# New planner settings for attention scores, value products and feed-forward sums past the opening

## The chip, the core and the metric

The kernel runs on one core of a Trainium2 chip. The metric is the device time of one execution in microseconds, the median of three runs. Beside it stands the profile of one execution, whose span runs from the first to the last instruction of the program.

## The reference

The program computes attention with normalised queries and keys and feeds the result into a multiplicative feed-forward network. There are 8 batches, 12 heads, 448 positions and 64 numbers per head; inputs are float32.

```
q_n = q / rms(q) * g_q ;  k_n = k / rms(k) * g_k
scores = q_n @ k_n.T / 8 ;  attn = softmax(scores) ;  o = attn @ v        # per head
x = o, with the 12 heads of a token side by side                          # 3584 x 768
h = (x @ w1) * (x @ w2) @ w3                                              # 3584 x 1024
out = h @ w_out                                                           # 3584 x 768
```

Nothing but a matrix product follows the multiplication of the two products, so the kernel computes w3 @ w_out once, calls it `w34s`, and multiplies by it.

## The kernel before

**Units of attention.** The work is cut into 24 units i of four heads each, three units to a batch. A unit goes through these steps. Its q and k are loaded (`load_qk`, L367, into one of three buffers). ScalarE squares them (`sq`, L464), VectorE sums the squares (L471), ScalarE takes a logarithm and an exponential for the inverse root (L480, L483), VectorE scales q and k by it (`scale`, L494; `by_g`, L503). For units 0 to 4 TensorE transposes the result; from unit 5 on a DMA issued by SyncE does it (`send`, L561). Then come seven score steps (`do_score`, L679): four 64x64-tile matmuls of 448 columns into two PSUM banks each, and one exponential on ScalarE over both banks (L701). I write S9.2 for step 2 of unit 9 on TensorE, and E9.2 for its exponential. When all seven exponentials of a unit, or of two units together, are done and v has landed, the value products run (`start_pv`, `do_pv_rest` L745, `do_pv_main` L766): per unit one sum of weights, whose reciprocal ScalarE takes as a logarithm and an exponential (`pv_summed`, L788 and L789), and two blocks of values, which VectorE multiplies by that reciprocal into `xT` (L808).

**Feed-forward.** When three units have filled `xT` of a batch, eight pairs of sums are queued for it: products with w1 (here A) and with w2 (here B). An A pair is copied to SBUF by ScalarE or VectorE (`half`, L352 or L358); the B pair is multiplied by that copy on VectorE (L949, into `abT`). The tiles of two batches are then multiplied by `w34s` (here O) and copied out and stored. A pair holds two PSUM banks and consists of twelve (A, B) or sixteen (O) passes; a pass (`do_pass`, L868) is four matmuls of 64x64 tiles that run side by side. Halfway through a pair the two row halves of the array swap banks. Before that swap a small instruction on SyncE or GpSimd (`hand_over`, L852) must have seen the first half end; if no other pass or score stands between the halves, TensorE waits for it.

**What sets the order.** The kernel is written by a planner while it is built. `Planner.run` keeps an estimated clock for each engine and a list of jobs with a duration, a key and conditions; on each engine the job that can start first, and among those the one with the lowest key, is written next. TensorE's next step is chosen by `pe_try`: value products first if `pv_size` allows them and enough banks are idle, then the running pair, a score if ScalarE is near the end of its work (`hungry`), a new pair if fewer than the permitted number are open (`next_pair`). Loads are jobs too: q and k of unit i+3 are issued once unit i is scaled, in SyncE's queue from unit 6 on, v by GpSimd (`load_v`, L407) when the queues are quiet. Once the kernel is built, each engine runs its list in that order, with semaphores between them; the planner's clocks are gone.

**Names that the change touches.** `MAX_PAIRS` limits open pairs, `PV_BANKS` is the number of idle banks for a double value product, `MARGIN` is how long before the present a bank must have come free to be preferred, `LOW`, `SOON`, `STARVED`, `HUNGRY`, `ONE`, `STOCK` and `PACE` are thresholds of `pv_size`, `score_ready` and `pe_try`, `QUAD` spaces the keys of successive units, `THIN`, `QUIET` and `LATE` belong to the loads.

Of the kernel before, what the change touches and what calls it, by code (L numbers as in the profile page):

```python
# [19 lines left out]
INF = float("inf")  # L20
# [4 lines left out]
LAG = {"ACT": 0.11, "DVE": 0.09, "SP": 0.0, "POOL": 0.0}  # L25
AHEAD = {"SP": 2.0, "POOL": 1.6}
AFTER = 0.7
LATE = 0.3
BUSY = 75.0


# [164 lines left out]
def kernel(  # L196
# [21 lines left out]
    NU = 2 * NF + 1  # L218
# [5 lines left out]
    CF = DFF // 128  # L224
# [15 lines left out]
    QUAD = 13.0  # L240
    WARM = 15
    WARM_TO = 13.0
    WARM_N = 256
    MAX_PAIRS = 2
    MARGIN = 0.25
    LOW = 2
    PV_BANKS = 6
    HOLD = 0
    SOON = 0
    STARVED = 4  # L250
    HUNGRY = 0.6
    ONE = 0
    PARTS = ((2, 4, 6, 8), (2, 4, 6, 8), (4, 8))
    EARLY_PAIRS = 3
    AHEAD_W3 = 4
    EARLY = 4
    STOCK = 14
    PACE = 1.7
    POOL_ORDER = (
        "o0 w0 w1 w2 o1 o2 o3 q1 v0 w3 w4 q2 w5 a0 v1 w6 w7 v2 a1 v3 q3 a2 b0 b1 q4 q5 b2".split()  # L260
    )
    ON_POOL = (1, 2, 3, 4, 5)
    IN_PARTS = (6, 7, 8)
    FIRST = 3.5
    THIN_FROM, THIN = 8, 2.5
    QUIET = 0.5

    w1s = const.tile([128, CM, DFF], BF, name="w1s")
    w2s = const.tile([128, CM, DFF], BF, name="w2s")
# [44 lines left out]
    ps_all = psum.tile([NP, 8, 512], FP, name="ps_all")  # L314

    plan = Planner()
    free, add = plan.free, plan.add


# [14 lines left out]
    w_at = {"w3": [INF] * CF, "w3T": [INF] * CF, "w_out": [INF] * 4, "w1": [INF] * NQB, "w2": [INF] * NQB}  # L334
    w34_at = []
# [5 lines left out]
    def all_of(times, n):  # L341
        return max(times) if len(times) == n else INF
# [29 lines left out]
    def plan_load_qk(i, key=None):  # L372
        eng, queue = (nc.gpsimd, "POOL") if i in ON_POOL else (nc.sync, "SP")

        def thin():

            left = sum(x[1] for x in plan.moving["SP"])
            return 0.0 if i < THIN_FROM or left < THIN else INF

        parts = 2 if i in IN_PARTS else 1  # L380
        for which in range(2):
            got = []

            def done(t, which=which, got=got):
                got.append(t)
                landed[i]["qk"[which]] = all_of(got, parts)

            for n in range(parts):
                x0, x1 = 2 * n // parts, 2 * (n + 1) // parts
                add(  # L390
                    queue, {"SP": 0.4, "POOL": 0.75}[queue],
                    (QUAD * i - 30 if key is None else key) + which * 0.01 + n * 0.001,
                    lambda which=which, x0=x0, x1=x1: load_qk(i, which, eng, x0, x1),
                    needs=[lambda: qk_free[i % 3] + (1.0 if i > 5 else 0.0), thin],
                    done=done, moves=(1.35 / parts, 0.086),
                )
# [58 lines left out]
    def plan_prep(i):  # L455
        s = st[i]
        pe = i < N_PE_T
        key = QUAD * i
        src = qk_bufs[i % 3]

        def sq(t, x0, x1):
# [169 lines left out]
    next_score = [0]  # L631
    last_score = [0.0]
    out_scores = [0]
# [12 lines left out]
    def score_ready(t):  # L646
        n = next_score[0]
        if n >= NQ * NU:
            return False
        i, g = divmod(n, NU)  # L650
        if g == 0 and min(p_free(x, i) for x in range(4)) > t:
            return False
        stock = sum(p.name != "w" for p in waiting)
        if stock >= STOCK and t < last_score[0] + PACE:
            return False
        return max(qkT_at[i]) + SEM <= t

    def do_score(t, z):
        n = next_score[0]
        next_score[0] += 1  # L660
        last_score[0] = t
        i, g = divmod(n, NU)
        s = st[i]
        if g == 0:
            x = min(range(4), key=lambda x: (p_free(x, i) > t, (x + 1) % 4))
            s["P"] = p_bufs[x]
            p_used[x] = i
            s["Pr"] = p_pool.tile([NP, 2, S], BF, tag="Pr", name="Pr")
        took = pass_us(S) + into("n")
        qkT, sc = s["qkT"], ps_all[:, z : z + 2]  # L670
        for c in range(2):
            if g < 2 * NF:
                pr, blk = divmod(g, NF)
                j = blk if c == pr ^ i % 2 else J + blk
            else:
                pr, j = c ^ i % 2, NF
            cols = slice(HP * pr, HP * pr + HP)
            for u in range(2):
                nc.tensor.matmul(  # L679
                    out=sc[HP * c : HP * c + HP, u, 0:S].rearrange(  # L680
                        "p (j s) -> p j s", j=NJ
                    ),
                    lhsT=qkT[u * D : (u + 1) * D, 1, j, cols],
                    rhs=qkT[u * D : (u + 1) * D, 0, :, cols],
                    start=True, stop=True, tile_position=(u * D, HP * c),
                )
        dst = (
            s["P"][:, pr::2, blk, :] if g < 2 * NF else s["Pr"]
        )
        bank_at[z] = bank_at[z + 1] = INF  # L690
        out_scores[0] += 1

        def done(e):
            bank_at[z] = bank_at[z + 1] = e + SEM
            out_scores[0] -= 1
            p_at[i].append(e + SEM)

        at = t + took + TO_ENGINE - pass_us(S) + 0.187
        add(
            "ACT", 0.80, QUAD * i + 1.8 * g,  # L700
            lambda: nc.scalar.activation(out=dst, in_=sc[:, :, 0:S], func=AF.Exp),  # L701
            needs=[lambda: at - 0.187], done=done,
        )
        if g == NU - 1:
            qkT_used[i] = t + took + 0.2
        return took
# [10 lines left out]
    def pv_size(t):  # L717


        i = next_pv[0]  # L720
        if not pv_one(i, t):
            return 0
        if i + 1 >= NQ:
            return 1
        if pv_one(i + 1, t):
            return 2
        if next_score[0] >= (i + 2) * NU - SOON:
            return 0
        if i == 1:
            return 0  # L730
        stock = sum(p.name != "w" for p in waiting)
        return 1 if stock < LOW or all_of(w34_at, CF) > t else 0

    def value_weights(i, hd, j, kind):
        if kind:
# [85 lines left out]
    pairs = []  # L821
    waiting = []
# [224 lines left out]
            for bb in {2 * t // NJ, (2 * t + 1) // NJ}  # L1047
        )

    last_x = [0]  # L1050

    def do_last(t, z):

# [107 lines left out]
        return took  # L1161

    def next_pair(t):
        if len(pairs) >= (EARLY_PAIRS if w_at["w_out"][3] == INF else MAX_PAIRS):
            return None
        return next((p for p in waiting if p.ready() <= t), None)

# [14 lines left out]

    def pe_step(t):

        took = pe_try(t, t - MARGIN)
        took = pe_try(t, t) if took is None else took
        if took is None and t < WARM_TO and idle_banks(t):
            return do_warm(single(idle_banks(t)))
        return took
# [51 lines left out]
    def pe_try(t, r):  # L1241
        idle = idle_banks(r)
        if pv_state:
            took = pv_state[0](t, idle)
            if took is not None:
                pv_state.pop(0)
            return took
        size = pv_size(r)
        if mode[0] == "v" and len(idle) >= 1 and size == 1:
            return start_pv(t, 1, idle)  # L1250
        last = HOLD and pairs and not any(p.ready() <= r for p in waiting)
        if size == 2 and len(idle) >= PV_BANKS and not last:
            return start_pv(t, 2, idle)
        two = adjacent(idle)
        score = score_ready(r) and out_scores[0] < 2 and two is not None and size != 2
        low = sum(p.name != "w" for p in waiting) < STARVED
        hungry = free["ACT"] <= t + (HUNGRY if low else 0.3) and out_scores[0] <= (
            ONE if low else 0
        )
        if mode[0] == "t":  # L1260
            took = any_turn(t, r, idle, 1)
            if took is not None:
                return took
        if running[0] and running[0].ready() <= r:
            if score and hungry:
                return do_score(t, two)
            return do_pass(running[0], t)
        took = any_turn(t, r, idle, 1 if w_at["w_out"][3] == INF else 2)
        if took is not None:
            return took  # L1270
        new = next_pair(r)
        late = [p for p in pairs if p.ready() <= r]
        if score:
            left = [z for z in idle if z not in (two, two + 1)]
            if hungry or late or new is None or adjacent(left) is not None:
                return do_score(t, two)
        if late:
            return do_pass(late[0], t)
        if size == 1 and len(idle) >= 2:
            return start_pv(t, 1, idle)  # L1280
        if two is not None and new is not None and not size:
            waiting.remove(new)
            start_pair(new, two)
            return do_pass(new, t)
        if next_pv[0] == NQ and not waiting and not pairs and last_x[0] < 2 and two is not None:
            if tile_at(B // 2 - 1, NT - 1) + SEM <= r:
                return do_last(t, two)
        return any_turn(t, r, idle, 1)
# [125 lines left out]
```

## Time and profile before

| | before |
|---|---|
| median of three runs | 354.11 us (353.96 to 354.86) |
| span of the profiled execution | 352.2 us |
| TensorE busy in it | 344.3 us, 98% |
| ScalarE busy in it | 261.9 us, 74% |
| VectorE busy in it | 206.8 us, 59% |
| GpSimd busy in it | 76.9 us, 22% |

Only the span is known of the profiled execution; the median lies 1.9 us above it, which is what lies around the span, and the two are kept apart below. The share of busy time counts a matmul from its start to a modelled end, and matmuls overlap, so a lost fraction of a microsecond hardly shows in it. The starts of successive matmuls show it: they follow each other at a fixed pace unless something is waited for.

### The profile page before, as it was taken

How to read it: one execution, taken by the hardware profiler on the slowest of the kernel's cores; microseconds unless marked ns; L12 is line 12 of the kernel's file. 1: busy time of each engine (PE TensorE's matmuls, PEld its weight loads, DVE VectorE, ACT ScalarE, POOL GpSimd, SP SyncE). 2: the span in 40 equal slices, each digit the busy share in tenths (PEclk: the TensorE clock that was granted, in tenths of full speed). 3: DMA queues.
4: the chain of work that ended last, by engine and by line, in shares of the span. 5: the costliest groups of instructions: out<-in, count | busy, mean ns of one | idle time of the engine just before them, and what ended most of it. 6: DMA issues, size and time to landing. Idle time of an engine off the chain costs nothing.

```text
span 352.2 us, 16197 instructions
## 1 busy us (share of the span) xinstructions
PE 344.3 (98%) x7374; PEld 225.6 (64%) x7374; DVE 206.8 (59%) x293; ACT 261.9 (74%) x375; POOL 76.9 (22%) x134
## 2 busy tenths in 40 slices
PE   8999999999999999999999999999999999999995
PEld 3766656657655756569856575565665656666674
DVE  5379377997989287894969758566643321222100
ACT  4779979989899989897889898777876942222122
POOL 8366720304212223113041031330130000000000
PEclk9999999999999999999999999999999999999998
DMA  8999999599997999988998879852690014100054
GB/s 198 240 273 190 236 306 246 102 184 259 197 202 171 200 160 238 208 161 182 203 247 142 215 102 252 218 72 38 116 176 6 4 47 108 33 2 2 5 165 151
DMA packets 68488, 55.11 MB, mean 156 GB/s; under 512 B 45060, under 2 KB 62372, under 8 KB 68420
## 3 DMA queue, kind: packets, MB, share of 16 engines
q1 hardware_dynamic: 49440, 35.33, 43.4%
q0 software_dynamic: 18048, 16.92, 27.8%
q10 hardware_dynamic: 932, 1.84, 1.5%
q8 instruction: 57, 0.93, 1.1%
q14 instruction: 11, 0.09, 0.1%
HBM read 46.66 MB, written 11.01 MB: 164 GB/s over the span
## 4 chain that ended last, share of the span: by engine, by line
PE 79%; DMA 7%; ACT 5%; DVE 4%; SPq 2%; issue 2%; POOL 2%; DVEq 0%; POOLq 0%; ACTq 0%
PE ps_all L868 59%; PE ps_all L766 9%; PE ps_all L679 8%; DMA w_outs<-in_moe_w_out_dram 3%; ACT P L701 2%; DMA qk_sb<-in_k_dram 2%; PE ps_all L745 2%; DMA qk_sb<-in_q_dram 2%; DVE qks L494 1%; DVE xT L808 1%; PE ps_all L1064 1%; ACT sq L464 1%; ACT half L352 1%; POOL w_outs L448 1%; SPq L561 1%
## 5 line engine op out<-in xcount | busy, mean ns | idle before, releaser
L701 ACT ACTIVATE P<-ps_all 128x896 bf16<-128x896 f32 x114 | 99.4, 922 | 12.0 <-PE ps_all L679 11.6
L407 POOL DMA_DIRECT2D v_sb<-in_v_dram x96 | 57.2, 616 | 177.6 <-PE ps_all L679 90.1
L868 PE MATMUL ps_all<-xT,w2s 64*64 64x448 bf16 x1536 | 89.0, 349 | 0.9 <-DVE xT L808 0.4
L868 PE MATMUL ps_all<-xT,w1s 64*64 64x448 bf16 x1536 | 89.1, 349 | 0.1
L868 PE MATMUL ps_all<-w34s,abT 64*64 64x384 bf16 x1728 | 80.5, 323 | 0.0
L352 ACT ACTIVATE half<-ps_all 128x896 bf16<-128x896 f32 (+1 forms) x38 | 33.3, 877 | 49.4 <-PE ps_all L868 49.3
L949 DVE TENSOR_TENSOR abT<-ps_all,half 128x896 bf16<-128x896 f32 x32 | 34.9, 1089 | 54.8 <-PE ps_all L868 54.6
L868 PEld LDWEIGHTS <-abT 64*64 64x64 bf16 x1728 | 55.1, 107 | 17.3 <-issue 0.7
L868 PEld LDWEIGHTS <-w2s 64*64 64x64 bf16 x1536 | 48.6, 107 | 25.9 <-issue 1.8
L868 PEld LDWEIGHTS <-w1s 64*64 64x64 bf16 x1536 | 47.7, 107 | 25.0 <-POOLq L852 0.9
L679 PE MATMUL ps_all<-qkT 64*64 64x448 bf16 x672 | 62.3, 352 | 0.8 <-ACT Pr L701 0.4
L471 DVE TENSOR_REDUCE ssq<-sq 128x14 f32<-128x896 f32 (+1 forms) x50 | 51.3, 1041 | 18.6 <-ACT sq L464 18.6
L494 DVE TENSOR_TENSOR qks<-qk_sb,al 128x448 bf16<-128x448 f32 x96 | 55.9, 618 | 1.4 <-ACT al L483 1.4
L464 ACT ACTIVATE sq<-qk_sb 128x896 f32<-128x896 f32 (+1 forms) x50 | 45.3, 922 | 2.4 <-DMA qk_sb<-in_k_dram 1.2
L808 DVE TENSOR_TENSOR xT<-ps_all,r 128x448 bf16<-128x448 f32 x48 | 27.7, 618 | 13.2 <-ACT r L789 10.3
L679 PEld LDWEIGHTS <-qkT 64*64 64x64 bf16 x672 | 23.2, 106 | 14.2 <-issue 4.9
L868 PE MATMUL ps_all<-w_outs,w3T 64*64 64x384 bf16 x512 | 25.1, 323 | 0.8 <-DVE w3T L358 0.5
L701 ACT ACTIVATE w_outs<-ps_all 128x896 bf16<-128x896 f32 x24 | 21.6, 912 | 5.2 <-PE ps_all L679 4.8
L766 PE MATMUL ps_all<-P,v_sb 128*32 128x448 bf16 x456 | 25.0, 352 | 0.0
L766 PEld LDWEIGHTS <-v_sb 128*32 128x32 bf16 x592 | 15.8, 97 | 12.2
L701 ACT ACTIVATE Pr<-ps_all 128x896 bf16<-128x896 f32 x24 | 22.1, 921 | 0.1
L358 DVE COPY half<-ps_all 128x768 f32<-128x768 f32 x13 | 12.4, 955 | 13.9 <-PE ps_all L868 13.2
(65 smaller groups left out, 212.8 us busy)
## 6 DMA issues: line engine op xcount, KB each, us to landing
out_dram<-half SPq DMA_DIRECT2D x48, 192.0 KB, 3.4
qk_sb<-in_q_dram SPq DMA_DIRECT2D x15, 448.0 KB, 5.0
qk_sb<-in_k_dram SPq DMA_DIRECT2D x15, 448.0 KB, 4.9
v_sb<-in_v_dram POOLq DMA_DIRECT2D x48, 64.0 KB, 3.8
v_sb<-in_v_dram POOLq DMA_DIRECT2D x48, 48.0 KB, 4.1
qk_sb<-in_q_dram POOLq DMA_DIRECT2D x5, 448.0 KB, 12.3
qk_sb<-in_k_dram POOLq DMA_DIRECT2D x5, 448.0 KB, 12.4
w3s<-in_moe_w_dram POOLq DMA_DIRECT2D x8, 256.0 KB, 6.9
```

Source lines behind the costliest of these rows:

```text
L352: nc.scalar.activation(out=out, in_=in_, func=AF.Copy, scale=1.0 if by is None else by)
L358: nc.vector.tensor_copy(out=out, in_=in_)
L407: nc.gpsimd.dma_start(out=v_bufs[i % 4][p0 : p0 + HP, g::2, 0 : j1 - j0].rearrange("p h j d -> p h (j d)"), in_=src[:, g::2, j0:j1].rearra ...
L464: nc.scalar.activation(out=s["sq", t][:, x0:x1], in_=src[:, t, x0:x1], func=AF.Square)
L471: nc.vector.tensor_reduce(out=s["ssq"][:, t, x0:x1], in_=s["sq", t][:, x0:x1], axis=AX, op=ADD)
L494: nc.vector.tensor_tensor(out=s["qks"][:, t, :, x], in0=src[:, t, x], in1=s["alpha"][:, t, x].unsqueeze(2).broadcast_to([NP, NJ, D]), op=MULT,
L679: nc.tensor.matmul(out=sc[HP * c : HP * c + HP, u, 0:S].rearrange("p (j s) -> p j s", j=NJ), lhsT=qkT[u * D : (u + 1) * D, 1, j, cols], rh ...
L701: lambda: nc.scalar.activation(out=dst, in_=sc[:, :, 0:S], func=AF.Exp),
L766: nc.tensor.matmul(out=ps_all[hd * HALF : (hd + 1) * HALF, z, 0:S], lhsT=value_weights(i, hd, j, kind), rhs=s["P"][:, hd, j, :] if j < NF ...
L808: lambda: nc.vector.tensor_tensor(out=xT[b][:, 2 * m + kind - 1, :], in0=ps, in1=s["r"], op=MULT),
L868: mm = nc.tensor.matmul(out=ps_all[64 * h : 64 * h + 64, p.bank + z, 0 : p.n], lhsT=lhsT[64 * r : 64 * r + 64, 64 * h : 64 * h + 64], rhs= ...
L949: nc.vector.tensor_tensor(out=abT[bp][:, f0 : f0 + 2, odd * S : (odd + 1) * S], in0=ps_all[:, z : z + 2, 0:S], in1=a_sb[b, f0], op=MULT,)
```

## The change

The thresholds become pairs of values, the first for the opening and the second from the planner's microsecond 55 on (`phase`). In the second phase three pairs may be open where it was two, a double value product starts with five idle banks where it took six, and the thresholds for banks, scores and exponentials have other values. The keys of the units after the sixth lie 12.284 apart where it was 13. Each time a score could be written, a counter `asked` goes up, and at eighteen listed counts (`AGAINST`) the score is held back for this once. Three settings of the loads change too: `THIN_FROM` and `THIN` (when a load of q and k may be queued), `QUIET` (when a load of v may be) and `LATE` (by how much a landing is taken to be late). No matmul, exponential, load or store is added or taken away; the lists of the engines are written in another order.

```diff
-LATE = 0.3
+LATE = 0.261
...
-    MAX_PAIRS = 2
-    MARGIN = 0.25
-    LOW = 2
-    PV_BANKS = 6
+    PAIRS = (2, 3)
+    MARGINS = (0.25, 0.241)
+    LOWS = (2, 4)
+    VALUE_BANKS = (6, 5)
     HOLD = 0
-    SOON = 0
-    STARVED = 4
-    HUNGRY = 0.6
-    ONE = 0
+    SOONS = (0, 1)
+    STARVES = (4, 4)
+    HUNGERS = (0.6, 0.989)
+    ONES = (0, 0)
+    FULL = (0.3, 0.3)
...
-    STOCK = 14
-    PACE = 1.7
+    STOCKS = (14, 14)
+    PACES = (1.7, 1.833)
+    SWITCH = 55.0
+    LATER = 12.284
+    KEYS = (1.8, 1.978)
+    AGAINST = (29, 31, 38, 41, 76, 86, 145, 155, 224, 229, 233, 235, 236, 245, 247, 260, 287, 329)
...
-    THIN_FROM, THIN = 8, 2.5
-    QUIET = 0.5
+    THIN_FROM = 7
+    THIN = 2.952
+    QUIET = 0.1
...
+    def phase():
+        return int(plan.now >= SWITCH)
+
+    def quad(i):
+        return QUAD * min(i, 6) + LATER * max(i - 6, 0)
...
-            "ACT", 0.80, QUAD * i + 1.8 * g,
+            "ACT", 0.80, quad(i) + KEYS[phase()] * g,
...
-        if len(pairs) >= (EARLY_PAIRS if w_at["w_out"][3] == INF else MAX_PAIRS):
+        if len(pairs) >= (EARLY_PAIRS if w_at["w_out"][3] == INF else PAIRS[phase()]):
...
-        if size == 2 and len(idle) >= PV_BANKS and not last:
+        if size == 2 and len(idle) >= VALUE_BANKS[phase()] and not last:
             return start_pv(t, 2, idle)
         two = adjacent(idle)
         score = score_ready(r) and out_scores[0] < 2 and two is not None and size != 2
...
+        if score:
+            asked[0] += 1
+            if asked[0] in AGAINST:
+                score = False
```

The other edits put `[phase()]` behind a threshold or `quad(i)` in the place of `QUAD * i`.

More of the change, by code (lines that the diff above doesn't have):

```diff
@@ L391, in plan_load_qk @@
                     queue, {"SP": 0.4, "POOL": 0.75}[queue],
-                    (QUAD * i - 30 if key is None else key) + which * 0.01 + n * 0.001,
+                    (quad(i) - 30 if key is None else key) + which * 0.01 + n * 0.001,
                     lambda which=which, x0=x0, x1=x1: load_qk(i, which, eng, x0, x1),
@@ L457, in plan_prep @@
         pe = i < N_PE_T
-        key = QUAD * i
+        key = quad(i)
         src = qk_bufs[i % 3]
@@ L653, in score_ready @@
         stock = sum(p.name != "w" for p in waiting)
-        if stock >= STOCK and t < last_score[0] + PACE:
+        if stock >= STOCKS[phase()] and t < last_score[0] + PACES[phase()]:
             return False
@@ L726, in pv_size @@
             return 2
-        if next_score[0] >= (i + 2) * NU - SOON:
+        if next_score[0] >= (i + 2) * NU - SOONS[phase()]:
             return 0
@@ L731, in pv_size @@
         stock = sum(p.name != "w" for p in waiting)
-        return 1 if stock < LOW or all_of(w34_at, CF) > t else 0
+        return 1 if stock < LOWS[phase()] or all_of(w34_at, CF) > t else 0
     def value_weights(i, hd, j, kind):
@@ L1048, in tile_at @@
         )
-    last_x = [0]
+    last_x, asked = [0], [0]
     def do_last(t, z):
@@ L1183, in pe_step @@
     def pe_step(t):
-        took = pe_try(t, t - MARGIN)
+        took = pe_try(t, t - MARGINS[phase()])
         took = pe_try(t, t) if took is None else took
@@ L1255, in pe_try @@
         score = score_ready(r) and out_scores[0] < 2 and two is not None and size != 2
-        low = sum(p.name != "w" for p in waiting) < STARVED
-        hungry = free["ACT"] <= t + (HUNGRY if low else 0.3) and out_scores[0] <= (
-            ONE if low else 0
+        if score:
+            asked[0] += 1
+            if asked[0] in AGAINST:
+                score = False
+        low = sum(p.name != "w" for p in waiting) < STARVES[phase()]
+        hungry = free["ACT"] <= t + (HUNGERS[phase()] if low else FULL[phase()]) and out_scores[0] <= (
+            ONES[phase()] if low else 0
         )
```

## The prediction

> **What bounds the kernel now.** I read the engine totals, the 40 slices, the waits, and then the timeline where matmul starts are too far apart.
>
> ```profile
> PE 344.3 (98%) x7374; PEld 225.6 (64%) x7374; DVE 206.8 (59%) x293; ACT 261.9 (74%) x375; POOL 76.9 (22%) x134
> ...
> PE   8999999999999999999999999999999999999995
> ...
> ACT  4779979989899989897889898777876942222122
> ```
>
> TensorE is full in every slice; ScalarE is nearly so up to about 200 us and falls away after 290. So time can only come from TensorE's losses, and these must be read from starts. I took the start of each unit of four matmuls that run side by side. Undisturbed units follow at 0.189 us (448 columns) or 0.1625 us (384), and a unit before a change of tile pattern (pass or score to value product and back) lasts about 0.105 us more. The list has 1941 units (single ones in the opening), worth 335.7 us at their steady pace, and 52 pattern changes, 5.5 us. With 1.2 us before the first matmul and 4.1 us after the last, that is 346.5 us. The span is 352.2, so 5.7 us net are waits. Most sit in a few places:
>
> ```profile
> 104.23 0.11 PEld L868 LDWEIGHTS <-w2s 64*64 64x64 bf16 x4 [0.55 <-POOLq L852]
> ```
>
> ```profile
> 145.36 0.11 PEld L679 LDWEIGHTS <-qkT 64*64 64x64 bf16 x4 [0.41 <-DMA qkT<-qks]
> ...
> 146.25 0.52 PEld L868 LDWEIGHTS <-w1s 64*64 64x64 bf16 x16 [0.55 <-POOLq L852]
> ...
> 148.79 0.95 ACT L464 ACTIVATE sq<-qk_sb 128x896 f32<-128x896 f32 x1 [1.24 <-DMA qk_sb<-in_k_dram]
> ...
> 150.12 0.53 ACT L788 ACTIVATE r<-ps_all 128x448 f32<-128x448 f32 x1
> ...
> 152.15 0.53 PE L868 MATMUL ps_all<-xT,w2s 64*64 64x448 bf16 x2
> ...
> 153.05 1.29 PE L868 MATMUL ps_all<-xT,w2s 64*64 64x448 bf16 x21 [0.37 <-DVE xT L808]
> ```
>
> ```profile
> 184.73 0.95 ACT L464 ACTIVATE sq<-qk_sb 128x896 f32<-128x896 f32 x1 [0.37 <-DMA qk_sb<-in_q_dram]
> ...
> 185.63 0.55 PE L868 MATMUL ps_all<-xT,w1s 64*64 64x448 bf16 x8
> ...
> 186.53 1.33 PE L868 MATMUL ps_all<-xT,w2s 64*64 64x448 bf16 x24 [0.35 <-ACT Pr L701]
> ```
>
> The lines at 104.23 and 146.25 are swaps of row halves with no other pass between: 0.29 us lost each. At 145.36 it is a score whose transposed keys land late: 0.18. Then k of unit 15 arrives 1.24 us late for a square; both reciprocals (L788) stand behind it, VectorE frees the product banks late, and TensorE loses 0.22 at 151.3 and 0.72 at 152.2. In the last fence two units from 185.63 would end at 186.01; the next starts at 186.53, so 0.53 is lost, since an exponential stood behind a square with a late load. At 191.8 another 0.29 follows in its wake. Unlike these, two losses come from lists that are short of filler:
>
> ```profile
> 115.71 0.59 PE L679 MATMUL ps_all<-qkT 64*64 64x448 bf16 x8
> 116.73 0.38 PE L679 MATMUL ps_all<-qkT 64*64 64x448 bf16 x4 [0.43 <-ACT Pr L701]
> 117.15 1.17 PE L868 MATMUL ps_all<-w34s,abT 64*64 64x384 bf16 x24
> ```
>
> Three scores in a row (S9.0 to S9.2) wait for banks: 0.62, 0.23 and, just before, 0.10: 0.95 us. At 258.6 0.14 is lost, at 51.0 0.48.
>
> **What the Trainium skill says.** "TensorE: Matmul & The Clock Gate", Back-to-back issue gap, gives N/2.4 + 2.5 ns for a warm matmul: 189 and 162.5 ns, as the starts here show. "Perfetto Trace Analysis", Identifying the Most-Contended Engine, warns that matmul busy share is no measure of the roofline; so it is here. "PSUM — Partial Sum Buffer", Engine vs sequencer instructions, has the queues of ScalarE, VectorE and GpSimd strictly first in, first out; the square at 148.79 with the reciprocals behind it agrees. The same page, PSUM bank collisions, says different row tiles may not access one bank at once; this is why halves are handed over, at 0.29 us where nothing covers it.
>
> **The change part by part.** I laid the lists of the two built programs beside each other.
>
> *TensorE's content: nothing.* 7374 matmuls, the same 1941 units and again 52 pattern changes, so the steady part stays 335.7 + 5.5 us. The lists part at unit 264, at 38.1 us; the last 55 us (A, B and O pairs alone) have the same order. The 0.48 at 51.0 is kept.
>
> *Swaps without cover: minus 0.58.* Of 106 swaps, before has two past the opening with nothing between the halves, those at 104.2 and 146.2. After has none; the shortest distance there is two scores, 0.38 us.
>
> *The short place at unit 8 and 9: nothing.* It moves but stays. After reads S8.2 S8.3 B(6 passes) S8.4 S8.5 S8.6 S9.0 and then O. S9.0 takes the bank of that B pair: VectorE's multiply of 1.00 us (L949's spacing), 0.23 us until it sees the sums and 0.12 for release make 1.35 us, and three scores cover 0.57: 0.78 us lost. The same sum for before (multiply to first O, with three scores between) also gives 0.78, and the trace shows 0.95. I take 0.95 for both.
>
> *The transpose of unit 12: minus 0.18.* Its logarithm stood behind E10.4 and now stands behind E10.0, so its transposes move forward from about 8 to 10 us of TensorE's list before S12.0. Before, the second landed 7.1 us after its issue (138.2 to 145.3).
>
> *The square of unit 15: minus 0.94.* SyncE's queue read: transpose of unit 12, two stores, second transpose, q 15, k 15. Now it reads: both transposes, q 15, two stores, k 15, all of it earlier, and the load of k has moved from 4 to 9 us of TensorE's list before the square. Its slowest issue to landing before was 7.2 us (141.54 to 148.7). The product after value units 10 and 11 now also starts in a bank freed earlier by a copy.
>
> *The square of unit 19: minus 0.82 (0.53 + 0.29).* Before, four stores stood between the two transposes of unit 16, so the second (1.8 us at 177.46) held the load of q 19 until 179.3, and it landed at 184.7. After, both transposes stand ahead of the stores. The square also stands one exponential later. I expect about 2 us of margin.
>
> *ScalarE: three copies fewer (35 for 38), VectorE three more (44 for 41).* 3 x 0.80 us and 3 x 1.0 us, off the path by themselves. But ScalarE is the tight engine from E8.1 to E12.0: 28 exponentials x 0.80, 5 squares x 0.84, 4 logarithm pairs x 0.48, two reciprocals x 1.04, two copies x 0.80 make 32.1 us (spacings of back-to-back instructions in the trace), against 30.8 us of TensorE's list there. Before it was 33.9 against 33.6. The 1.3 us over are covered by the lag of one or two exponentials that the banks allow, and by the 0.95 just lost; about 0.3 us is left. If ScalarE's spacing is a few per cent longer, TensorE pays. I bound this between 0 and 0.8 and take 0.2.
>
> *Other landings: between 0 and 2, I take 0.2.* Each load of q and k stands at least 7 us of list ahead of its square (unit 12 is closest, 102 against 109.5), and the usual landing of a full load is 5 us. Loads of v are at least 10 us ahead. A new late one isn't visible in any list, so it is bounded by two events of the size of unit 15's.
>
> Sum: 0.58 + 0.18 + 0.94 + 0.82 = 2.52 us less, 0.4 us given back: 2.1 us. The span becomes 350.1, and with the 1.9 us that separates the median from the span, 352.0 us.
>
> **Rivals.** *Late loads move (around 354, no change).* Before lost most of its time to loads that came 0.4 to 1.2 us after their squares. If the new order has as many such meetings in other places, 1.5 to 2.5 us come back: 353.5 to 354.5. For it: the queues carry the same bytes. Against: the distances above have grown at each place that failed.
>
> *ScalarE becomes the bound from 111 to 142 us (slower).* There the queue no longer empties, so each stop of ScalarE on a load passes to TensorE, less 0.3 us of cover. To be slower by 1.1 us the stops must reach 2.5 + 1.1 + 0.3 = 3.9 us. That takes a load that needs over 11 us from issue to landing, for unit 12 or 13; loads that competed with the weights in the opening did take 12.3. It would give about 355.5. Against: of the loads past 60 us whose landing the trace shows none took more than 7.2.
>
> *The short place is filled after all (faster still).* If S9.0 and the O tiles lose nothing, because VectorE frees the bank sooner than I reckon, another 0.9 us goes: 351.0.
>
> *The order does not matter.* Planner settings that leave the list alike can't move time; but the lists do part, and the swaps without cover are gone by construction, so at least 0.6 us should show.
>
> **How the numbers follow.** Gains gone as summed, up to 0.8 given back: 0.62, at 352.0. Filled short place: 0.09. Late loads moved: 0.18. ScalarE bound and slower: 0.11. A measurement here tells 0.3%, 1.06 us, from no change. Faster than 353.05 takes the first two and a bit of the third: 0.75; same 0.14; slower than 355.17 0.11. The range that leaves 2 in 10 out runs from 351.0 (the filled place) to 354.6 (the end of moved loads). The first case alone covers 351.4 to 352.8.
>
> **What would show it right or wrong.** In the new profile the waits of TensorE's weight loads on GpSimd's small instruction should be shorter, and no square near units 15 or 19 should wait for its load; TensorE should run without loss from 118 to 200 us, and one loss of about 0.9 us should stand near 113, now at S9.0 and the O passes behind it. Wrong would be: ScalarE without idle time from 111 to 142 and exponentials releasing TensorE there, a square near unit 12 or 13 behind a load, or a reciprocal behind one.

## The result and the profile after

| | before | after |
|---|---|---|
| median, both measured side by side | 354.03 us (353.12 to 354.86, 6 runs) | 351.94 us (350.84 to 352.43, 6 runs) |
| span of the profiled execution | 352.2 us | 349.7 us |
| waits of TensorE over its steady pace, net | 5.7 us | 3.2 us |

The changed kernel takes 0.994 of the time before, with a 95% interval of 0.9922 to 0.9958. That is 2.1 us less. One execution of the changed kernel differs from another by up to 1.6 us, so the two profiles stand for one execution each. The whole span difference, 2.5 us, is found again in the waits: 1941 units and 52 pattern changes are the same in both, so the steady 341.2 us did not move. The median before lies between 353.85 and 354.37 in the comparisons below, so those compare by ratio.

The page after, in the lines that were read before: the totals of the engines and the 40 slices.

```profile
PE 342.6 (98%) x7374; PEld 221.3 (63%) x7374; DVE 210.2 (60%) x296; ACT 259.9 (74%) x372; POOL 76.8 (22%) x134
...
PE   8999999999999999999999999999999999999995
...
ACT  4779979979999999998699898667876842222122
```

They hardly differ from the page before: TensorE's busy share is again 98%, and only its sum fell, by 1.7 us. In ScalarE's row the nines now follow each other without a break for nine slices (79 to 157 us), where before eights stood between them: it has less slack there. The gain shows only in the starts. This is the loss over the steady pace by stretch of the span, worked out from the starts of TensorE's units as in the prediction (negative values come from the opening, where single units are quicker than their price):

| us of the span | 0–10 | 10–38 | 38–100 | 100–120 | 120–160 | 160–200 | 200–250 | 250–290 | 290– |
|---|---|---|---|---|---|---|---|---|---|
| before | −1.16 | 1.59 | 0.71 | 1.35 | 1.71 | 1.01 | 0.12 | 0.27 | 0.11 |
| after | −1.32 | 1.55 | 0.68 | 0.84 | 0.31 | 0.10 | 0.70 | 0.27 | 0.11 |

From 100 to 200 us 2.8 us went; from 200 to 250 0.6 came back.

Timeline of ScalarE after, at unit 15 and at unit 19, the two places whose squares waited for a load before. Columns are start, duration, engine, line, operation, operands and count; a bracket names idle time and what ended it.

```profile
144.73 1.79 ACT L477 ACTIVATE sq<-qk_sb 128x896 f32<-128x896 f32 x2
...
147.90 0.54 ACT L801 ACTIVATE r<-ps_all 128x448 f32<-128x448 f32 x1 [0.46 <-PE ps_all L779]
...
182.15 0.91 ACT L714 ACTIVATE Pr<-ps_all 128x896 bf16<-128x896 f32 x1
182.95 0.95 ACT L477 ACTIVATE sq<-qk_sb 128x896 f32<-128x896 f32 x1
183.79 0.92 ACT L714 ACTIVATE P<-ps_all 128x896 bf16<-128x896 f32 x1
```

No square has a bracket. The sign to look for is the one at 147.90: the reciprocal, which stood behind a late square before, is now early and waits for TensorE. The order of that meeting has turned round.

Timeline of TensorE after, at units 8 and 9:

```profile
113.34 1.30 PE L881 MATMUL ps_all<-xT,w2s 64*64 64x448 bf16 x24
114.47 1.06 PE L692 MATMUL ps_all<-qkT 64*64 64x448 bf16 x12
115.84 0.38 PE L692 MATMUL ps_all<-qkT 64*64 64x448 bf16 x4 [0.31 <-DVE abT L962]
116.03 1.98 PE L881 MATMUL ps_all<-w34s,abT 64*64 64x384 bf16 x44
```

Three scores from 114.47 should end at 115.04, and S9.0 starts at 115.84: 0.80 us lost. The release is VectorE's multiply (L962), as expected.

The new losses past 200 us. First SyncE's queue, then ScalarE, both timelines of after:

```profile
213.53 5.52 SPq L574 DMA_TRANSPOSE qkT<-qks  x2
219.10 0.57 SPq L380 DMA_DIRECT2D qk_sb<-in_q_dram  x1
```

```profile
224.32 0.95 ACT L477 ACTIVATE sq<-qk_sb 128x896 f32<-128x896 f32 x1 [1.17 <-DMA qk_sb<-in_q_dram]
225.18 0.90 ACT L714 ACTIVATE P<-ps_all 128x896 bf16<-128x896 f32 x1
```

Two transposes took 5.52 us of the queue where other pairs of this execution took 2.6 to 3.6 us; the load of q 23 behind them came 1.17 us late for its square. The exponential behind that square ended at 226.08, and the score that waits for it started at 226.13: TensorE lost 0.15 us.

Between 218 and 226 TensorE lost 0.57 us in all, but the other 0.42 (0.26 inside a value product at 218.0 and 0.16 at the score behind it) was lost some 4 us before this square was due, so the load cannot be its cause. Timelines of TensorE and of its weight loads:

```profile
217.47 0.74 PE L779 MATMUL ps_all<-P,v_sb 128*32 128x448 bf16 x12
218.04 1.18 PE L779 MATMUL ps_all<-w_outs,v_sb 128*32 128x448 bf16 x12
```

```profile
218.49 0.85 PEld L779 LDWEIGHTS <-v_sb 128*32 128x32 bf16 x20 [0.53 <-issue]
```

Two steps of equal work take 0.74 and 1.18 us, and "issue" means that the profile shows nothing that was waited for. The profile does list a queue that it names "instruction"; this is the page's line for it, with transfers, MB and share:

```profile
q8 instruction: 57, 0.93, 1.1%
```

A 16 KB transfer of this queue began at 216.20, and TensorE went on 2.29 us later. Two runs below with the same list of TensorE up to here (one pair in the last stretch, halved multiply) stop at the same matmul and go on 2.31 and 2.29 us after the start of that transfer. In three others (load of k 15 put back, both together, changed again) it began 2.42 to 2.66 us ahead of the matmul, and nothing was lost. The 0.16 follows in the three traces with the stop alone. So here TensorE seems to have waited for its next instructions; no run tested this.

### The profile page after: what moved, and what is told of

Its sections match the earlier page's. It is cut to its first block, busy times and chain, and to the rows that moved or that the text cites. A ratio compares the mean times of both kernels' runs of the same rounds, so it can differ in the third digit from the quotient of the medians.

```text
span 349.7 us, 16194 instructions
## 1 busy us (share of the span) xinstructions
PE 342.6 (98%) x7374; PEld 221.3 (63%) x7374; DVE 210.2 (60%) x296; ACT 259.9 (74%) x372; POOL 76.8 (22%) x134
## 4 chain that ended last, share of the span: by engine, by line
PE 85%; ACT 8%; DVE 3%; issue 2%; DMA 1%; ACTq 0%; SPq 0%
PE ps_all L881 62%; PE ps_all L779 12%; PE ps_all L692 8%; ACT P L714 3%; PE ps_all L758 2%; ACT half L714 1%; ACT Pr L714 1%; DVE qks L507 1%; ACT sq L477 1%; DMA qk_sb<-in_q_dram 1%; PE ps_all L1077 1%; PE ps_all L1136 1%; DVE w34s L371 1%; ACT w_outs L714 1%; ACT w34s L365 0%
## 5 line engine op out<-in xcount | busy, mean ns | idle before, releaser
L881 PE MATMUL ps_all<-xT,w1s 64*64 64x448 bf16 x1536 | 88.1, 349 | 0.0
L881 PE MATMUL ps_all<-xT,w2s 64*64 64x448 bf16 x1536 | 87.3, 349 | 0.0
L365 ACT ACTIVATE half<-ps_all 128x896 bf16<-128x896 f32 (+1 forms) x35 | 30.7, 877 | 50.2 <-PE ps_all L881 50.2
L962 DVE TENSOR_TENSOR abT<-ps_all,half 128x896 bf16<-128x896 f32 x32 | 34.8, 1088 | 51.5 <-PE ps_all L881 49.9
L881 PEld LDWEIGHTS <-abT 64*64 64x64 bf16 x1728 | 52.8, 107 | 19.0 <-issue 0.4
L881 PEld LDWEIGHTS <-w2s 64*64 64x64 bf16 x1536 | 46.6, 107 | 25.3
L881 PEld LDWEIGHTS <-w1s 64*64 64x64 bf16 x1536 | 46.5, 107 | 25.2
L692 PE MATMUL ps_all<-qkT 64*64 64x448 bf16 x672 | 60.6, 352 | 0.6 <-DVE abT L962 0.3
L692 PEld LDWEIGHTS <-qkT 64*64 64x64 bf16 x672 | 22.0, 106 | 14.2 <-issue 5.1
L371 DVE COPY half<-ps_all 128x768 f32<-128x768 f32 x14 | 13.4, 957 | 13.9 <-PE ps_all L881 11.3
```

The lines of the kernel that those rows point to most:

```text
L365: nc.scalar.activation(out=out, in_=in_, func=AF.Copy, scale=1.0 if by is None else by)
L371: nc.vector.tensor_copy(out=out, in_=in_)
L692: nc.tensor.matmul(out=sc[HP * c : HP * c + HP, u, 0:S].rearrange("p (j s) -> p j s", j=NJ), lhsT=qkT[u * D : (u + 1) * D, 1, j, cols], rh ...
L881: mm = nc.tensor.matmul(out=ps_all[64 * h : 64 * h + 64, p.bank + z, 0 : p.n], lhsT=lhsT[64 * r : 64 * r + 64, 64 * h : 64 * h + 64], rhs= ...
L962: nc.vector.tensor_tensor(out=abT[bp][:, f0 : f0 + 2, odd * S : (odd + 1) * S], in0=ps_all[:, z : z + 2, 0:S], in1=a_sb[b, f0], op=MULT,)
```

## The experiments

Two things were settled by laying the lists of built programs beside each other, without running them. The two settings that the change is named after do nothing: with pairs and value banks set back to (2, 2) and (6, 6) the changed kernel gives the identical program on every engine, and the kernel before with only these two changed gives the program of before. What alters the list are `AGAINST`, `MARGINS`, `HUNGERS`, `PACES` and three settings of the loads (`LATE`, `THIN`, `QUIET`); `THIN_FROM`, `LOWS`, `SOONS`, `KEYS` and the new spacing of the keys, each set back alone, leave the program as it is. So the theory was put more narrowly: *most of the gain comes from where late loads stand in SyncE's queue.* Its rival: *TensorE's order and the bank hand-overs make most of it.*

**One queue alone.** In the kernel before, the stores that stood ahead of the loads of units 15 and 19 are issued behind them. Every other engine's list stays as before.

```diff
+        if i == behind[0] and which:        # in load_qk, after the load
+            behind[0] = 0
+            while held:
+                held.pop(0)()
...
         def send(t):
+            if i in (12, 16) and t == 0:
+                behind[0] = i + 3
...
             def store(x, eng=nc.sync):
+                if behind[0]:
+                    held.append(lambda: store_now(x, eng))
+                else:
+                    store_now(x, eng)
```

> The kernel before, with one thing changed: in SyncE's queue the two stores between the transposes of unit 12 stand behind the loads of unit 15, and the four between the transposes of unit 16 behind the loads of unit 19. TensorE's, ScalarE's and VectorE's lists stay as they are, word for word. My theory (late landings in SyncE's queue cost the 0.18, 0.94 and 0.82 us named in the prediction): about 1.9 us less, 352.1 us, and the squares of units 15 and 19 no longer wait. Rival (the loads are late whatever the queue's order, since the same bytes move): within 0.5 us of the kernel before. Rival (the new order of TensorE's list made the gain, not the loads): no change either.

Measured: 352.3 us (351.97 to 352.82), ratio 0.9929 (0.9904 to 0.9954), span 350.2. SyncE's queue, timeline of this kernel:

```profile
171.92 2.69 SPq L568 DMA_TRANSPOSE qkT<-qks  x2
174.70 1.26 SPq L368 DMA_DIRECT2D qk_sb<-in_q_dram  x1
176.06 0.42 SPq L368 DMA_DIRECT2D qk_sb<-in_k_dram  x1
176.57 2.88 SPq L1018 DMA_DIRECT2D out_dram<-half  x4
```

and of before at the same place:

```profile
173.46 1.25 SPq L561 DMA_TRANSPOSE qkT<-qks  x1
174.80 2.61 SPq L1005 DMA_DIRECT2D out_dram<-half  x4
177.46 1.82 SPq L561 DMA_TRANSPOSE qkT<-qks  x1
179.32 0.58 SPq L367 DMA_DIRECT2D qk_sb<-in_q_dram  x1
```

The load of q 19 is issued 4.6 us earlier. Net waits fell from 5.7 to 3.7 us, nearly all of it here: 1.71 to 0.50 from 120 to 160 us, 1.01 to 0.44 from 160 to 200. The losses of TensorE's own order stayed: the bare swaps at 103.5 (0.29) and 145.3 (0.32), and 0.95 at units 8 and 9.

One more stayed that the prediction had put down to the late square of unit 19: 0.292 us at 189.8 (191.8 before). Timelines of TensorE and of ScalarE in this kernel, where that square is not late:

```profile
189.80 0.39 PE L875 MATMUL ps_all<-xT,w1s 64*64 64x448 bf16 x4
190.28 0.57 PE L875 MATMUL ps_all<-xT,w2s 64*64 64x448 bf16 x8
```

```profile
188.48 2.56 ACT L708 ACTIVATE P<-ps_all 128x896 bf16<-128x896 f32 x3
```

The B pair that opens at 190.28 takes the banks of S15.4, written only at 188.86, and in the list its first matmul waits for that score's exponential, the second of these three (189.28 to 190.2). The loss belongs to TensorE's order.

The 0.18 at the first score of unit 12 is gone in this kernel too. So moving stores in one queue is enough for a gain of the size of the whole change. It does not show that the change got its gain by that route alone; the next two runs ask for its two halves.

**One load of the changed kernel put back.** The load of k 15 goes behind both transposes of unit 13.

```diff
+        if i == 15 and which and not held:
+            held.append(lambda: load_qk(i, which, eng, x0, x1))
+            return
...
+            if i == 13 and t == 1:          # in send, after the transpose
+                held[0]()
```

> The changed kernel, with one thing put back: the load of k of unit 15 stands behind both transposes of unit 13 in SyncE's queue, some 4 us later. All other lists stay. My theory: it lands 2 to 4 us after the slot of its square, the two reciprocals of units 10 and 11 wait behind it in ScalarE's queue, and TensorE loses 0.5 to 1.5 us at S12.1 and after it: 352.4 to 353.4 us. Rival (such waits of ScalarE hide behind TensorE's work): no change, 351.9 us.

Measured: 353.55 us, ratio 0.9975 (0.9956 to 0.9993), against 0.994 for the changed kernel; span 351.3. Timeline of ScalarE:

```profile
148.97 0.95 ACT L481 ACTIVATE sq<-qk_sb 128x896 f32<-128x896 f32 x1 [2.90 <-DMA qk_sb<-in_k_dram]
...
150.63 0.54 ACT L807 ACTIVATE r<-ps_all 128x448 f32<-128x448 f32 x1
```

and of TensorE:

```profile
152.25 0.38 PE L698 MATMUL ps_all<-qkT 64*64 64x448 bf16 x3 [0.69 <-ACT r L807]
```

The chain of before is back: late load, square, reciprocals behind it, TensorE waits. Of 2.9 us that the square waited TensorE lost 1.7 (0.21 at 150.7, 0.86 at 151.2, 0.60 at 154.2). One load's place is worth 1.2 us by the ratios; their intervals just touch, so the trace is the stronger evidence.

**The price of a bare swap.** Once the last value product is written, only one pair may be open, so that each of the 24 pairs of the last stretch swaps its row halves with nothing between.

```diff
-        if len(pairs) >= (EARLY_PAIRS if w_at["w_out"][3] == INF else PAIRS[phase()]):
+        if len(pairs) >= (EARLY_PAIRS if w_at["w_out"][3] == INF else 1 if next_pv[0] == NQ else PAIRS[phase()]):
```

> The changed kernel, with only one pair of sums open once the last value product is written, so that its two halves follow each other: 24 swaps of row halves then have no other pass between them. The work is the same. My theory, with 0.29 us for each as in the trace of the kernel before: 7.0 us more, 358.9 us. Rival (the 0.29 us was GpSimd's queue being busy at those two places, and a bare swap costs little): under 2 us more.

Measured: 359.95 us (two runs), ratio 1.0143 (1.0091 to 1.0194), span 358.6. The waits of this kernel (us in total, times, longest):

```profile
PEld L881 <- POOLq L865: 12.7, 24, 0.6
```

Each wait of a weight load is 0.50 or 0.55 us long, but TensorE's next start is late by 0.291 to 0.293 us, 24 times over: 7.0 us. The weight load ran ahead of its matmul, which is why its wait is the longer. The other 1.8 us by which this span exceeds the changed kernel's lie elsewhere; the largest pieces are 0.62 us at 185.5, 0.6 more in the first 38 us and 0.3 more at the stop near 219. The loss at 185.5 is of interest, since up to the last stretch this list is that of the changed kernel:

```profile
184.51 0.95 ACT L477 ACTIVATE sq<-qk_sb 128x896 f32<-128x896 f32 x1 [0.84 <-DMA qk_sb<-in_q_dram]
```

In this execution q 19, issued at 177.33, took 7.2 us to land and came late again.

**The multiply at units 8 and 9.** The last multiply of batch 1 does one bank; the other half of its output is a copy of the A product, made earlier, so half of that multiplication is left out.

```diff
+            if i == 12 and t == 0:
+                nc.vector.tensor_copy(
+                    out=abT[0][:, CF - 1, S : 2 * S], in_=a_sb[1, CF - 2][:, 1]
+                )
...
+                y = 1 if (b, f0) == (1, CF - 2) else 2
                 nc.vector.tensor_tensor(
-                    out=abT[bp][:, f0 : f0 + 2, odd * S : (odd + 1) * S],
-                    in0=ps_all[:, z : z + 2, 0:S],
-                    in1=a_sb[b, f0],
+                    out=abT[bp][:, f0 : f0 + y, odd * S : (odd + 1) * S],
+                    in0=ps_all[:, z : z + y, 0:S],
+                    in1=a_sb[b, f0][:, 0:y],
```

> The changed kernel, with the last multiply of batch 1 taking one bank instead of two (the other half of the result is a copy of the A product, so this half of the multiplication is left out), which shortens that instruction from about 1.09 to about 0.6 us. My theory (S9.0 waits for the bank that this multiply frees): the loss at S8.6 and S9.0 falls from 0.80 to about 0.3 us, the time by 0.5 at most. Rival (ScalarE's exponentials set the loss there): 0.80 stays.

Measured in one run: 352.26 us, span 350.5. The multiply took 0.62 us instead of 1.09, but TensorE still lost 0.69 us instead of 0.80, where 0.3 was expected. Timeline of TensorE:

```profile
114.56 1.28 PE L696 MATMUL ps_all<-qkT 64*64 64x448 bf16 x16
116.05 1.17 PE L885 MATMUL ps_all<-w34s,abT 64*64 64x384 bf16 x24 [0.20 <-ACT w_outs L718]
```

and of ScalarE:

```profile
112.95 0.31 ACT L497 ACTIVATE lnv<-ssq,eps_t 128x28 f32<-128x28 f32 x1
113.29 0.23 ACT L500 ACTIVATE al<-lnv 128x28 f32<-128x28 f32 x1
113.46 3.35 ACT L718 ACTIVATE w_outs<-ps_all 128x896 bf16<-128x896 f32 x4
```

The expectation that VectorE alone holds this place fell. S9.0 now comes sooner and the O passes wait instead, for exponentials that run back to back behind a logarithm pair. The two causes are 0.11 us apart: without the multiply the exponentials hold the place. In this execution, too, the load of q 19 was late (issued at 177.65, its square waits 0.75 us, TensorE loses 0.53 at 184.9).

**Both together.** The changed kernel, with stores put behind the loads of units 15, 19 and 23 as in the first experiment.

```diff
+            if i in (12, 16) and t == 0:    # in send; the rest as in the first experiment
+                behind[0] = i + 3
...
+        if i == 22 and which:               # in load_qk, after the load
+            behind[0] = 23
```

> The changed kernel, with SyncE's queue alone altered as in the run before: stores stand behind the loads of units 15, 19 and 23 where they stood ahead. My theory (what is left past unit 12 is again late loads: 0.57 us near 218 to 226 in the changed kernel's trace, and 0.6 us at S15.2 in some executions): 0.6 to 0.9 us less than the changed kernel, 351.1 us. Rival (these waits come from the memory traffic of that moment, not from the place in the queue): no change, 351.9 us.

Measured: 351.73 us (351.13 to 352.44, 12 runs), ratio 0.9928 (0.9905 to 0.9951), span 349.9. The interval overlaps that of the changed kernel, so no further gain is shown. From 160 to 200 us only 0.09 us is lost, but 0.31 at 219.5. Timelines of SyncE's queue and of ScalarE:

```profile
210.83 0.46 SPq L381 DMA_DIRECT2D qk_sb<-in_k_dram  x1
```

```profile
217.56 0.95 ACT L484 ACTIVATE sq<-qk_sb 128x896 f32<-128x896 f32 x1 [1.48 <-DMA qk_sb<-in_k_dram]
```

The load of k 22, with no store close ahead of it, took up to 6.7 us. At 218 us the order of the queue was not the cause; what slowed this load stays open.

**The settings apart.** Three kernels split the change: the new load settings in the kernel before; the changed kernel with the old load settings; the changed kernel without the list of scores that are held back.

```diff
-LATE = 0.3
+LATE = 0.261
...
-    THIN_FROM, THIN = 8, 2.5
-    QUIET = 0.5
+    THIN_FROM, THIN = 7, 2.952
+    QUIET = 0.1
```

> The kernel before with the three settings of the loads alone (LATE, THIN with THIN_FROM, QUIET). Its list of TensorE has one swap without cover (0.29 us), the short place at unit 9 (about 1.0), two smaller short places (0.17 and 0.4), the same 52 pattern changes, and a load of q of unit 18 only 5 us of list ahead of its square. My theory (a list's losses can be added up before it runs): past 100 us about 2.1 us lost where the kernel before loses 4.5: 351.9 us with the change of both settings not needed. Rival (the thresholds of pairs, scores and exponentials made the gain): 354.0 us or more.

Measured: 354.13 us, ratio 1.0005 (0.9978 to 1.0032), span 352.2: no gain at all where about 2 us was expected from reading the lists. The losses near 145 and 186 are gone, but q loads of other units come late. Timeline of ScalarE:

```profile
218.35 0.95 ACT L464 ACTIVATE sq<-qk_sb 128x896 f32<-128x896 f32 x1 [0.58 <-DMA qk_sb<-in_q_dram]
...
227.75 0.95 ACT L464 ACTIVATE sq<-qk_sb 128x896 f32<-128x896 f32 x1 [1.24 <-DMA qk_sb<-in_q_dram]
```

From 213 to 231 us 1.7 us is lost. About half of it follows from these loads: 0.35 us at 219.6 and 0.37 at 229.0, each where TensorE waits for the exponential behind the late square, and 0.14 soon after. This half is what the rival of moved loads described. But 0.53 us goes at 213.3, where a value product waits for an exponential and ScalarE had met no late load for 20 us; that is TensorE's order. For 0.30 us at 220.3 the profile names no releaser.

The reverse, old load settings in the changed kernel, is the same diff turned round.

> The changed kernel with the settings of the loads as before. Its list has one more pattern change (0.66 us), two swaps without cover (0.58), the short place at unit 9 (0.8), one of 1.06 near 154 and 0.4 near 201, and a load of q of unit 19 only 5 us ahead of its square. My theory: about 2.3 us more than the changed kernel, 354.2 us, as slow as the kernel before. Rival (thresholds of pairs, scores and exponentials made the gain): 351.9 us.

Measured: 355.9 us, ratio 1.0043 (1.0022 to 1.0063), span 354.3; 354.2 had been expected. TensorE lost 1.13 us at 159.5, where a value product waits for a multiply (L962) to free its bank, 0.94 at 117 to 118, and 0.46 at 208; 0.29 each at 252.0 and 345.8; and about 1.5 us more than in the changed kernel went from 10 to 38 us, 1.0 of it at 18 us, where a load of `w_out` lands late. So a part of this result is a late landing of the opening and not the order past it.

```diff
-    AGAINST = (29, 31, 38, 41, 76, 86, 145, 155, 224, 229, 233, 235, 236, 245, 247, 260, 287, 329)
+    AGAINST = ()
```

> The changed kernel with the list of held-back scores emptied. Its list has one more pattern change and three more units (0.66 us), one swap without cover (0.29), the short place at unit 9 (0.8) and a second one of 0.86 before the value products near 154. My theory (losses add up): 1.4 us more than the changed kernel, 353.3 us. Rival (the held-back scores are noise of a search and change nothing): 351.9 us.

Measured: 354.28 us, ratio 1.0011 (0.9987 to 1.0036), span 351.7; 353.3 had been expected. The largest loss is again a value product that waits for a multiply (timeline of TensorE):

```profile
157.84 0.38 PE L758 MATMUL ps_all<-Pr,ones 64*32 64x448 bf16 x8
158.98 0.57 PE L758 MATMUL ps_all<-Pr,v_sb 64*32 64x448 bf16 x16 [0.77 <-DVE abT L962]
```

Neither half of the change gives the gain alone, and taking either away loses about all of it. In these runs the settings work as a set; of those that alter the list, not every one was run alone. The losses added up for these three lists before they ran came out 1.0 to 2.2 us too low.

**The changed kernel again.** The same kernel, run once more, and beside it a variant meant to be the best: one score fewer held back (entry 76), the loads' settings a little changed (`THIN` 2.995, `QUIET` 0.41), and stores behind the loads of units 15 and 19.

> The changed kernel itself once more, for a second trace of the same lists. My theory (what is left of its waits past 160 us are landings that differ between executions): the short place at unit 9 shows the same 0.8 us to 0.01, while the losses near 185 (S15.2) and 218 to 226 differ by more than 0.2 us from the first trace; the time is 0.6% below the kernel before. Rival (all losses belong to the list): every place as in the first trace.

> The changed kernel with one held-back score fewer, slightly other thresholds for the loads (THIN 2.995, QUIET 0.41), and stores behind the loads of units 15 and 19 in SyncE's queue: the load of q of unit 19 then stands 15 us of list ahead of its square instead of 9, and the list has no swap without cover. My theory: no loss from 125 to 200 us in any execution, so 0.3 us less than the changed kernel on average, 0.7% below the kernel before. Rival (nothing is left to gain there): as the changed kernel.

Measured: changed again 352.34 us (350.91 to 354.02), ratio 0.9953 (0.9931 to 0.9975), profiled span 349.1. The variant 351.96 us, ratio 0.9942 (0.9923 to 0.9961), span 349.7. The variant is not distinguishable from the changed kernel.

The repeat is the more instructive. Its losses at units 8 and 9 are 0.295 and 0.503 us, those of the first trace to about a thousandth. The 0.57 us at 218 to 226, the stop inside the value product included, is absent (0.09 from 200 to 250 us), although the square of q 23 was late here as well, by less; timeline of ScalarE:

```profile
223.46 0.95 ACT L477 ACTIVATE sq<-qk_sb 128x896 f32<-128x896 f32 x1 [0.79 <-DMA qk_sb<-in_q_dram]
```

So 0.79 us of lateness cost TensorE nothing and 1.17 us cost 0.15: the cover lies between. Near 185 nothing was lost in either trace, so there the expected difference did not come. In these traces losses by TensorE's own order recur, and losses by late loads, like the stop at 218, differ between executions of one program. Net waits were 2.6 us here against 3.2.

## Why the prediction was right

The time, 351.9 us, is at the forecast of 352.0, and the mechanism is the one forecast: swaps without cover and late loads gone, the rest nearly kept. That it agrees to a tenth is luck: executions of the changed kernel lie between 350.8 and 354.0, its second median is 352.3, the same way of adding up missed three kernels of the experiments by 1.0 to 2.2 us, and one step below had two parts wrong that did not show in the sum.

*Steady part unchanged: right.* The same units, the same pattern changes, and the span difference equals the difference of the waits. The pace needs a word: the section of the Trainium skill that the prediction takes it from ("TensorE: Matmul & The Clock Gate", Back-to-back issue gap) gives its formula for an isolated matmul and says that it counts too much for a sustained stream of wide ones. Here the sustained stream kept it, 0.189 us at 448 columns, with four tiles side by side; the measured starts are what the sum rests on.

*Swaps without cover, minus 0.58: right.* Both losses of 0.292 us are gone, and the price holds: 24 times in the one-pair kernel.

*Transpose of unit 12, minus 0.18: right.* The loss of 0.177 at the first score of unit 12 is gone. The prediction names the earlier logarithm as its cause; the first experiment, which leaves ScalarE's list alone, removes the loss as well, so the place in SyncE's queue is enough, and what the logarithm adds is not shown.

*Square of unit 15, minus 0.94: right, cause shown.* Its two losses (0.22 and 0.72) are gone; the first experiment removes them by SyncE's queue alone, the second brings the chain back with one load.

*Square of unit 19, minus 0.82 (0.53 + 0.29): the sum came true in both traces of the changed kernel, but two parts of the step were wrong.* First, the 0.29 said to follow in the late square's wake does not: it stays in the first experiment, where the square is on time, and is a wait for a bank that the new order of TensorE avoids. Second, the margin. The prediction gave about 2 us, from a usual landing of 5. In the changed kernel the load was issued at 176.51, landed 6.3 us later and was 0.2 us ahead of its square at 182.95. In two other executions with nearly the same list it took 7.2 and 6.2 us from a somewhat later issue, the square waited 0.84 and 0.75, and TensorE lost 0.62 and 0.53. The margin of 2 us is not there; the 0.53 is gained in some executions and not in others, and that both traces of the changed kernel have it is luck. With the loads ahead of the stores (first experiment, both together, and the last variant) the square was on time in each of the three traces.

*The short place, nothing: sized 0.95, measured 0.80.* Its own sum had given 0.78; the adjustment to 0.95, taken because before had measured 0.95 against the same sum, was the error. The chain named (VectorE's multiply of 1.00 us) is the one that released S9.0, but exponentials were 0.11 us behind it, which the sum did not hold, and which the halved multiply showed.

*ScalarE tight, 0.2 lost (0 to 0.8): about right* (the terms as printed make 32.2 us, not 32.1). The change has one new loss in that stretch, 0.177 us at 123.7, where TensorE turns from units 8 and 9's O passes to a value product while ScalarE is busy without a break. That ScalarE is its cause is read from the timeline and not shown by a run.

*Other landings, 0.2 lost (0 to 2): 0.15 in the first trace, behind the square of q 23, nothing at that place in the second.* The step was right to leave it open. What it did not foresee is the other 0.42 us of that stretch, which no landing explains.

So of the 2.51 us that went at named places, 1.64 (0.18 + 0.94 + 0.53) hung on transfers in SyncE's queue and 0.88 (twice 0.29 and the 0.29 at 191.8) on TensorE's order. The sum of the named gains was 2.52 us less 0.4. Measured between the first traces, the named places gave 2.51 and the short place 0.15 more; 0.18 and 0.57 came back; that is 1.9. Another 0.55, to reach 2.47, is spread over pieces too small to name, 0.16 of it in the first 10 us.

Of the rivals, moved loads were real: the new load settings in the old kernel have the gain at units 15 and 19 and lose most of it again at 213 to 231, about half of that by late loads. The changed kernel escaped it for the most part. The rival's premise, that before lost most of its time to late loads, was too strong: they account for 1.64 of 5.7 us. ScalarE did not become the bound. The short place was not filled. That the order does not matter is refuted by the changed kernel without held scores, which loses the gain.

## What to carry to other kernels

When an engine is 98% busy, compare the starts of its instructions with their steady pace, list the places that lose, and follow each to what released it; the busy shares of two kernels 2 us apart look alike. A late transfer is often late because something unhurried stands ahead of it in its own issuing queue, here four stores (2.6 us together) and a second transpose: lay the queue's list beside the consumers' before changing the busy engine's order. Judge a margin by the slowest landing seen in several executions, not by the usual one, and repeat a trace before believing a loss that a load causes. Check too that the late load comes before the loss that it is blamed for: 0.42 of 0.57 us near 218 were lost before the load was due.

## What was not expected of the hardware

A swap of row halves with nothing between cost 0.291 to 0.293 us in each of 24 swaps in one run, of products with different operands and widths of 384 and 448 columns; a single one in the first experiment cost 0.315. Two transposing DMAs in SyncE's queue took from 2.6 us to 5.5 us (5.52 in one execution of the changed kernel at 213 us and 4.66 in the other, with the same list around them). Some loads of q and k past 135 us landed 6.2 to 7.7 us after their issue, where the usual full load took about 5; what makes them slow there is not known. In three traces TensorE stood still inside a value product, waiting for nothing that the profile shows, until 2.29 to 2.31 us after the start of a transfer of instructions.
